# Lower limit and integer sums of a weight conversion moved from VectorE to GpSimd, first pair's phase 1 in other PSUM tiles, and a new order of left-over products

One core of one Trainium2 chip. The metric is the device time of one execution in microseconds (us); lower is better.

## The reference, cut

Cross attention between 8 x 512 tokens and 8 x 32 state rows, then a feed-forward layer with the gate h cos(h):

```python
def _moe_ref(x, w_in, w_out):          # x: 4352 x 512, w_in: 512 x 2048
    h = x @ w_in
    g = h * np.cos(h)
    return (g @ w_out).astype(np.float32)

def reference(**kwargs):               # ... cut: inputs split by name
    attn_out = _attn_ref(**attn_kwargs)        # softmax(x state^T) state, and back
    x = attn_out.transpose(0, 2, 1, 3).reshape(B * S, H * D)
    return _moe_ref(x=x, **moe_kwargs)
```

## The kernel before

The weights arrive as 64-bit floats. A load of 128 x 1024 values is rebuilt as 32-bit floats in parts named by letters: "1" and "2" on ScalarE, then the lower limit "a", the shift "b", the sign "c" and the integer sum "d".

```python
def convert_part(i, p):
    # ... cut: dst, bits (dst as int32), raw (64-bit source), e (low half)
    if p == "1":   nc.scalar.activation(dst, raw...[..., 1], func=ACTF.Abs)      # L206
    elif p == "2": nc.scalar.activation(e, raw...[..., 0], func=ACTF.Copy, ...)  # L209
    elif p == "a": nc.vector.tensor_scalar(dst, dst, 2.0 ** -15, None, op0=ALU.max)          # L212
    elif p == "b": nc.vector.tensor_scalar(bits, bits, 3, None, op0=ALU.logical_shift_left)  # L214
    elif p == "c": nc.vector.scalar_tensor_tensor(out=bits, in0=raw[..., 1], ...)            # L217
    else:
        engine = nc.vector if i < 4 else nc.gpsimd
        engine.tensor_tensor(bits, bits, e.bitcast(I32), op=ALU.add)                         # L223
```

The main loop has 144 steps of one hidden tile each; the first 128 belong to four pairs of batches, 32 steps to a pair, in four phases of eight. A step, cut:

```python
    hidden(t)                       # TensorE: h (L425)
    gate(t); gate2(t)               # ScalarE, then VectorE (L434)
    if conv >= 0: convert(conv, "1")
    # ... cut: attention work
    if conv >= 0: convert(conv, "a")
    gate3(t)                        # ScalarE: Abs, Sin
    gate4(t)                        # VectorE: h times cos(h), the gate product (L446)
    sums(t)                         # VectorE: subtractions for later products (L452)
    if conv >= 0: convert(conv, "2"); convert(conv, "bcd")
    output(line.pop(0))             # TensorE: products of the tile of three steps ago (L490)
```

A pair's output products are sums over eight tiles in one of two pairs of PSUM tiles, MAIN and SIDE (PSUM is the memory that TensorE's products are summed in). At the end of phase 2, MAIN is copied out by ScalarE (L501) and VectorE (L503); phase 3 begins with a new sum in MAIN, and TensorE may have to wait for the copies. That place is called a pair's jam below. The left-over products of the pair before (`more`) use SIDE and fill TensorE meanwhile. The weights s1 to s4 are sums and differences of blocks of `w_out`, made once by GpSimd; s2 and s4 stand for the products with them.

```python
        if t.phase == 3:
            if product(MAIN, s2, pr.b[0, i], i): ...   # wants MAIN at once
            free(pr.b[0, i])
            if product(SIDE, s4, t, i): ...            # wants SIDE
            free(t)
        elif pr.before and (t.phase * NH + i) % 3 < 2:
            pr.before.more(1)                          # 16 left-overs over phases 0 to 2
```

## Time and profile before

| | before |
|---|---|
| median of the first 3 executions | 836.75 us (834.78 to 836.91) |
| span of the profiled execution | 834.2 us |
| mean granted TensorE clock | 0.967 |

Two lines of the page of before, next to those that the prediction shows. In a profile, PE is TensorE's matmuls and PEld its weight loads, DVE is VectorE, ACT ScalarE and POOL GpSimd; the granted clock (PEclk) is the share of its full clock that TensorE was given. The first line has each engine's busy time, its share of the span and its number of instructions; the second line has GpSimd's busy tenths in 40 slices of about 21 us.

```profile
PE 775.2 (93%) x2720; PEld 349.1 (42%) x2720; DVE 463.3 (56%) x723; ACT 398.1 (48%) x644; POOL 99.4 (12%) x66
...
POOL 1033336776100000000000000000000000000200
```

GpSimd is busy 12% of the span, nearly all of it in the first eleven slices.

### The profile page before, as it was taken

What the parts mean: (1) busy time and instruction counts of PE and PEld (TensorE: products, weight loads), DVE (VectorE), ACT (ScalarE), POOL (GpSimd) and SP (SyncE); (2) the same over time, 40 slices, a digit from 0 to 9 for tenths busy, and PEclk for the clock granted to TensorE, in tenths of its full rate; (3) what the DMA queues carried; (4) which work ended last, traced back from release to release, by engine and by line L of the source; (5) the groups of instructions that cost most, each with busy time, mean ns of one, the idle gap of its engine ahead of it and who ended that gap; (6) DMA issues with size and microseconds to landing.
All of it is one profiled execution on the core that took longest, in us unless ns stands there. A gap on an engine that the chain in (4) does not pass through costs nothing.

```text
span 834.2 us, 7432 instructions
## 1 busy us (share of the span) xinstructions
PE 775.2 (93%) x2720; PEld 349.1 (42%) x2720; DVE 463.3 (56%) x723; ACT 398.1 (48%) x644; POOL 99.4 (12%) x66
## 2 busy tenths in 40 slices
PE   3589499989999999989999999899999999999997
PEld 2134144334434443434434344344444444355554
DVE  3889895662354446764455456853563455644331
ACT  1658775553437444634455445534363444322222
POOL 1033336776100000000000000000000000000200
PEclk9679989999999999989999999899999999999999
DMA  6584421102010211040011120130010110400121
GB/s 151 182 241 157 151 76 26 26 4 48 1 26 1 51 26 26 0 76 0 1 25 35 23 32 13 20 57 0 10 16 1 26 26 0 126 0 8 18 39 38
DMA packets 110500, 37.18 MB, mean 45 GB/s; under 512 B 102464, under 2 KB 102464, under 8 KB 110464
## 3 DMA queue, kind: packets, MB, share of 16 engines
q1 hardware_dynamic: 109248, 36.19, 18.6%
q10 hardware_dynamic: 1088, 0.26, 0.2%
q8 instruction: 21, 0.34, 0.2%
q0 software_dynamic: 128, 0.26, 0.2%
q14 instruction: 15, 0.12, 0.0%
HBM read 27.79 MB, written 8.91 MB: 44 GB/s over the span
## 4 chain that ended last, share of the span: by engine, by line
PE 76%; DVE 13%; ACT 7%; issue 1%; DMA 1%; POOL 0%; SPq 0%; DVEq 0%; POOLq 0%
PE o L490 41%; PE h L425 25%; PE at L277 4%; PE o L603 3%; DVE q L434 2%; ACT q L440 1%; DVE g_all L452 1%; DVE w_out L212 1%; PE at L250 1%; ACT q L439 1%; PE at L364 1%; DVE g_all L446 1%; DVE xT L297 1%; DMA x_b<-in_x_dram 1%; DVE w_out L217 1%
## 5 line engine op out<-in xcount | busy, mean ns | idle before, releaser
L425 PE MATMUL h<-aT,sw 128*128 128x512 f32 x512 | 247.0, 606 | 15.3 <-DVE g_all L446 9.4
L490 PE MATMUL o<-g_all,w_out 128*128 128x512 f32 x512 | 240.7, 606 | 9.8 <-ACT held L501 5.8
L431 ACT ACTIVATE q<-h 128x512 f32<-128x512 f32 (+1 forms) x144 | 82.4, 572 | 285.0 <-PE h L425 284.8
L434 DVE SCALAR_TENSOR_TENSOR q<-q,h 128x512 f32<-128x512 f32 (+1 forms) x144 | 94.4, 656 | 201.7 <-ACT q L431 201.6
L490 PE MATMUL o<-g_all,s 128*128 128x512 f32 x384 | 184.4, 616 | 8.2 <-ACT held L501 5.6
L446 DVE TENSOR_TENSOR g_all<-h,q 128x512 f32<-128x512 f32 (+1 forms) x144 | 94.9, 659 | 133.6 <-ACT q L440 133.4
L425 PEld LDWEIGHTS h<-aT,sw 128*128 128x128 f32 x512 | 98.9, 195 | 144.1 <-issue 115.5
L490 PEld LDWEIGHTS o<-g_all,w_out 128*128 128x128 f32 x512 | 94.7, 192 | 131.5 <-issue 122.3
L439 ACT ACTIVATE q<-q 128x512 f32<-128x512 f32 (+1 forms) x144 | 87.7, 609 | 103.2 <-DVE q L434 103.1
L490 PEld LDWEIGHTS o<-g_all,s 128*128 128x128 f32 x384 | 71.4, 195 | 102.9 <-issue 84.5
L440 ACT ACTIVATE q<-q,halfpi 128x512 f32<-128x512 f32 (+1 forms) x144 | 100.6, 699 | 4.5
L223 POOL TENSOR_TENSOR w_out<-w_out,s 128x1024 int32<-128x1024 int32 x10 | 23.6, 2359 | 603.9 <-DVE w_out L217 599.5
L452 DVE TENSOR_TENSOR g_all<-g_all 128x512 f32<-128x512 f32 x96 | 62.2, 688 | 1.6
L452 POOL TENSOR_TENSOR g_all<-g_all 128x512 f32<-128x512 f32 x32 | 40.0, 1276 | 26.2 <-DVE g_all L446 17.7
L425 PE MATMUL h<-sT,w_in 128*128 128x256 f32 x128 | 30.2, 379 | 0.0
L406 ACT COPY sw<-at 128x512 f32<-128x512 f32 x48 | 25.7, 589 | 9.0 <-PE at L277 9.0
L603 PE MATMUL o<-w_out,g_all 128*128 128x512 f32 x64 | 29.6, 592 | 0.0
L425 PEld LDWEIGHTS h<-sT,w_in 128*128 128x128 f32 x128 | 24.3, 190 | 10.1 <-issue 6.7
L496 DVE SCALAR_TENSOR_TENSOR held<-o,held 128x512 f32<-128x512 f32 x40 | 25.5, 682 | 4.3 <-PE o L490 4.3
L277 PE MATMUL at<-w_in,stT 64*32 64x512 f32 x384 | 26.1, 601 | 0.0
L517 DVE STREAM_TRANSPOSE ot<-held 128x512 f32<-128x512 f32 x32 | 22.3, 698 | 0.0
L223 POOL TENSOR_TENSOR w_in<-w_in,s 128x1024 int32<-128x1024 int32 x6 | 14.2, 2361 | 57.6 <-DVE w_in L217 57.6
(79 smaller groups left out, 456.1 us busy)
## 6 DMA issues: line engine op xcount, KB each, us to landing
out_dram<-ot SPq DMA_DIRECT2D x136, 64.0 KB, 2.0
x_b<-in_x_dram SPq DMA_DIRECT2D x32, 256.0 KB, 4.6
g_all<-in_moe_w_out_dram SPq DMA_DIRECT2D x8, 1024.0 KB, 5.0
g_all<-in_moe_w_in_dram SPq DMA_DIRECT2D x6, 1024.0 KB, 5.1
g_all<-in_moe_w_in_dram SPq DMA_DIRECT2D x4, 512.0 KB, 6.9
x_b<-in_moe_w_out_dram SPq DMA_DIRECT2D x1, 1024.0 KB, 6.0
xT<-in_moe_w_out_dram SPq DMA_DIRECT2D x1, 1024.0 KB, 8.1
s<-in_state_dram ACTq DMA_DIRECT2D x4, 64.0 KB, 5.3
```

The source lines that it names most:

```text
L223: engine.tensor_tensor(bits, bits, e.bitcast(I32), op=ALU.add)
L277: nc.tensor.matmul(out=(to or at)[j][Ns * k:Ns * k + Ns, 0:n], lhsT=w[D * j:D * j + D, self.b, Ns * k:Ns * k + Ns], rhs=r(slice(D * j, D * ...
L406: nc.scalar.copy(dst, to[j][:, 0:c1 - c0])
L425: nc.tensor.matmul(out=t.hp, lhsT=t.lhs(i), rhs=t.rhs(i), start=(i == 0), stop=(i == t.kn - 1))
L431: nc.scalar.activation(t.q, t.hp, func=ACTF.Copy, bias=MAGIC)
L434: nc.vector.scalar_tensor_tensor(out=t.q, in0=t.q, scalar=MAGIC, in1=t.hp, op0=ALU.subtract, op1=ALU.subtract)
L439: nc.scalar.activation(t.q, t.q, func=ACTF.Abs)
L440: nc.scalar.activation(t.q, t.q, func=ACTF.Sin, bias=halfpi, scale=-TWO_PI)
L446: nc.vector.tensor_tensor(t.g, t.hp, t.q, op=ALU.mult)
L452: engine.tensor_tensor(out, a, b, op=ALU.subtract)
L490: nc.tensor.matmul(out=acc[bank][ch], lhsT=w[:, i, P * ch:P * ch + P], rhs=g.g, start=(i == 0), stop=(i == NH - 1))
L603: nc.tensor.matmul(out=acc[MAIN][i], lhsT=t.g[:, P * i:P * i + P], rhs=w_out[:, :, t.f, :], start=(n == 0), stop=(n == NF - 1))
```

## The change

The intent is to relieve VectorE in the first 128 us, where it is full, and to shorten the waits of TensorE for PSUM at the start of phase 3. Three parts: (1) the lower limit and all integer sums go to GpSimd, which otherwise idles; (2) the first pair's phase 1 uses SIDE instead of MAIN, and the conversions are spread differently over the steps; (3) left-over products go first in a step and are spent earlier, and in phase 3 the product s4 (SIDE) goes ahead of s2 (MAIN).

```diff
         elif p == "a":
-            nc.vector.tensor_scalar(dst, dst, 2.0 ** -15, None, op0=ALU.max)
+            nc.gpsimd.tensor_scalar(dst, dst, 2.0 ** -15, None, op0=ALU.max)
...
-            engine = nc.vector if i < 4 else nc.gpsimd
-            engine.tensor_tensor(bits, bits, e.bitcast(I32), op=ALU.add)
+            nc.gpsimd.tensor_tensor(bits, bits, e.bitcast(I32), op=ALU.add)
...
+        if t.phase < 3 and pr.before and i % 3 < 2:
+            pr.before.more(1)
...
-            if product(MAIN, a12, t, i):
+            bank = MAIN if pr.before else SIDE
+            if product(bank, a12, t, i):
...
         if t.phase == 3:
-            if product(MAIN, s2, pr.b[0, i], i):
-            ... cut: sum with what is held
-            free(pr.b[0, i])
-            if product(SIDE, s4, t, i):
+            last = product(SIDE, s4, t, i)
+            free(t)
+            ... cut: sum with what is held
+            product(MAIN, s2, pr.b[0, i], i)
+            free(pr.b[0, i])
+            ... cut: sum with what is held
...
-        elif pr.before and (t.phase * NH + i) % 3 < 2:
-            pr.before.more(1)
...
-            prod(11, 0, 3, SIDE)
-            prod(13, 1, 0, SIDE)
+            prod(10, 0, 3, SIDE)
+            prod(13, 1, 0, MAIN)
...
-            prod(0, b, 1, *bank)
+            prod(0, b, 1, *[MAIN for _ in bank])
...
-    conv_at = {s: s + 4 for s in range(N_LOADS - 4)}
+    conv_at = {s: 4 + i for i, s in enumerate(
+        (0, 1, 2, 3, 4, 5, 6, 7, 8, 11, 12, 13, 14, 15))}
... cut: GpSimd's sums of weight blocks one or two steps later
```

More of the change, by code (lines that the diff above doesn't have):

```diff
@@ L574, in output @@
         if t.phase == 1:
-            if product(MAIN, a12, t, i):
+            bank = MAIN if pr.before else SIDE
+            if product(bank, a12, t, i):
                 o = Held()
                 for ch in range(2):
-                    plus(o, MAIN, ch, pr.u)
+                    plus(o, bank, ch, pr.u)
                 store(2 * pr.n, 0, o)
@@ L584, in output @@
         if t.phase == 3:
-            if product(MAIN, s2, pr.b[0, i], i):
-                for ch in range(2):
-                    plus(pr.u, MAIN, ch, pr.u)
-            free(pr.b[0, i])
-            if product(SIDE, s4, t, i):
+            last = product(SIDE, s4, t, i)
+            free(t)
+            if last:
                 o = Held()
@@ L592, in output @@
                     plus(o, SIDE, ch, pr.p5)
+            product(MAIN, s2, pr.b[0, i], i)
+            free(pr.b[0, i])
+            if last:
+                for ch in range(2):
+                    plus(pr.u, MAIN, ch, pr.u)
                 total(o, o, pr.u)
                 store(2 * pr.n + 1, 0, o)
-            free(t)
-        elif pr.before and (t.phase * NH + i) % 3 < 2:
-            pr.before.more(1)
     def state_output(t):
@@ L745 @@
     lo, hi = slice(0, NH // 2), slice(NH // 2, NH)
-    block_at = {13: (ALU.add, s1, a21, a22, lo),
-                15: (ALU.add, s1, a21, a22, hi),
-                17: (ALU.subtract, s2, s1, a11, lo),
-                18: (ALU.subtract, s2, s1, a11, hi),
-                19: (ALU.subtract, s4, a12, s2, lo),
-                20: (ALU.subtract, s4, a12, s2, hi),
+    block_at = {15: (ALU.add, s1, a21, a22, lo),
+                17: (ALU.add, s1, a21, a22, hi),
+                18: (ALU.subtract, s2, s1, a11, lo),
+                19: (ALU.subtract, s2, s1, a11, hi),
+                20: (ALU.subtract, s4, a12, s2, lo),
+                21: (ALU.subtract, s4, a12, s2, hi),
                 22: (ALU.subtract, s3, a11, a21, lo),
```

## The prediction

> **What bounds the kernel now.** I read the 40 slices first, for where TensorE is not full; then busy time in 20 us stretches, the groups by shape, the list of waits, and the timeline at each gap.
>
> ```profile
> PE   3589499989999999989999999899999999999997
> DVE  3889895662354446764455456853563455644331
> PEclk9679989999999999989999999899999999999999
> ...
> 80.00:100.00 20.00, 12.48 (x42) 4.58 (x40) 18.05 (x23) 13.74 (x20) 6.29 (x3) 1.00 0.41 143
> 100.00:120.00 20.00, 15.29 (x62) 6.70 (x63) 19.02 (x25) 16.24 (x23) 7.08 (x4) 0.74 0.29 104
> ```
>
> The columns of a stretch are PE, PEld, DVE, ACT, POOL, then clock, DMA share, GB/s. From about 128 us TensorE is full, with two dips (slices 17 and 26, 340-360 and 520-540 us) where the clock also falls. From 20 to 128 us VectorE is full instead: the weights arrive as 64-bit floats and are rebuilt there, one load a step. So only the first 128 us and the dips can yield; TensorE's matmuls themselves are not changed.
>
> ```profile
> L212 DVE TENSOR_SCALAR w_out<-w_out 128x1024 f32<-128x1024 f32 x10 | 16.0, 1598 | 1.9 <-ACT w_out L206 1.9
> L223 POOL TENSOR_TENSOR w_out<-w_out,s 128x1024 int32<-128x1024 int32 x10 | 23.6, 2359 | 603.9 <-DVE w_out L217 599.5
> L223 DVE CUSTOM_DVE_ANT_0 w_in<-w_in,s 128x1024 uint16<-128x1024 uint16 x4 | 2.8, 691 | 0.5 <-DVE w_in L217 0.2
> ...
> 80.33 0.65 DVE L212 TENSOR_SCALAR w_in<-w_in 128x1024 f32<-128x1024 f32 x1
> ...
> 118.41 2.37 POOL L223 TENSOR_TENSOR w_out<-w_out,s 128x1024 int32<-128x1024 int32 x1 [3.15 <-DVE w_out L217]
> 118.78 2.55 DVE L212 TENSOR_SCALAR w_out<-w_out 128x1024 f32<-128x1024 f32 x1
> ```
>
> The lower limit (L212) costs 0.65 us alone and 2.55 when the previous load's integer sum (L223) runs on GpSimd. A step without attention work takes 5.5 us (sums start at 72.00 and 77.53).
>
> ```profile
> PE o L490 <- ACT held L501: 11.4, 3, 5.8
> ...
> 104.05 2.05 PE L490 MATMUL o<-g_all,w_out 128*128 128x512 f32 x2 [5.80 <-ACT held L501]
> ...
> 352.54 1.28 DVE L496 SCALAR_TENSOR_TENSOR held<-o,held 128x512 f32<-128x512 f32 x2
> 356.85 2.08 PE L490 MATMUL o<-g_all,s 128*128 128x512 f32 x2 [2.79 <-ACT held L501]
> 358.40 0.68 DVE L503 TENSOR_SCALAR held<-o 128x512 f32<-128x512 f32 x1
> 359.14 4.78 PE L490 MATMUL o<-g_all,s 128*128 128x512 f32 x6 [0.21 <-DVE held L503]
> ```
>
> These three waits (the last column is the longest) are PSUM: a new sum wants the MAIN tiles before L501 and L503 copied the old one out. 104.05 is pair 0's phase 1, 356.85 pair 1's phase 3; the third (536.68) is pair 2's. Six matmul passes take 4.78 us here, 2.58 at full clock (0.43 each).
>
> **What the Trainium skill says.** "SBUF — State Buffer", section "Who interferes with whom": VectorE and GpSimd share a port pair under an exclusive lock, and a tensor_scalar in a 2-port mode waits for the whole GpSimd instruction. The trace agrees: L212 ends at 121.33, 0.55 after the sum's end at 120.78. "GPSIMD Engine Reference", section "Engine selection": two-input elementwise work is about twice as slow on GpSimd, one-input "roughly line-rate"; section "Elementwise — side-by-side cycle accounting" gives 1.03 cycles per element for a body that small. The first half agrees (512-wide subtraction 1.28 us on GpSimd, 0.69 on VectorE); the trace has no such one-input instruction of this size. "TensorE: Matmul & The Clock Gate", section "What's actually happening": half rate after an idle window of about 3.4 us. The trace agrees roughly: 2.8 us idle after 1.1 us of small matmuls halved the clock, gaps of 1.9 and 1.65 us (171.8, 712.3) did not.
>
> **Part 1, conversions.** VectorE loses 20 lower limits (16.0+7.2+1.6 = 24.8 us) and 4 sums (2.8); GpSimd gains them. Estimate of a GpSimd lower limit: 1024 x 1.03 / 1.2 GHz = 0.88 us plus 0.19 (the intercept of its sums: 1.276 at 512, 2.36 at 1024) = 1.07. The 24.8 us do not come off, because a loop forms: sum of load i, limit of i+1 (same in-order engine), shift, xor, sum of i+1. Its length: 2.36 + 1.07 + about 0.1 + 0.72 (shift start to xor start) + 1.36 (xor start to sum start, 70.64 to 72.00) = 5.6 us, against 5.5 now. So steps without attention gain nothing. Steps that VectorE's own sum sets do: shift to shift, load 11 came 7.44 us after load 10 (75.45 to 82.89) and becomes about 6.7; the next 6.71 minus 1.38 is below the loop, so 5.7. Start-up: the first sum is 0.6 us slower (1.28 for 0.69), but VectorE is freed of about 2 us ahead of the second softmax; I take -0.8.
>
> The conversions skip steps 9 and 10, and end in step 15 instead of 13. Steps 9 to 11 are set now by ScalarE's exponentials plus two conversions (gate products L446 at 87.81, 94.50, 102.43, 110.22). Without the latter: 8 to 9 about 4.8 (xor, then the chain L434, Abs, Sin, 2.1 us); 9 to 10 about 8 (the chain measured 7.62 at 336.58 to 344.20, plus the softmax sums); 10 to 11 about 4.5. That is 17.3 for 22.4. Then five loop steps at 5.7 end the last conversion near 130 us, where its sum started at 123.93 before, but the two 2.8 us steps that followed are now inside. Taken together, TensorE, which is full from 128.59 on, begins step 18's matmuls near 132.2 instead of 136.9: -4.4 us with start-up.
>
> **Part 2, first pair's phase 1 in SIDE.** It removes the 5.8 us wait at 104.05, but GpSimd, VectorE and ScalarE hold that stretch anyway: it is what lets part 1 show, and adds nothing to its sum.
>
> **Part 3, left-over products first, s4 before s2.** Nothing is added. Left-overs end at phase 2's fifth tile instead of its seventh, so L496 (1.28 us) leaves the jam before 356 us, and s4's four passes (1.72 us) stand between the old sum's end and the need for MAIN. Walking pair 1 with the measured durations: two of the left-overs come before step 56's matmuls that now come after, so step 55's gate is 1.7 us later, and with it the chain of 7.62 and 5.8 us behind it: the gate product of step 57 ends at 352.4 instead of 350.7. TensorE, now without filler, waits about 1.2 us for it, does the hidden matmuls (1.72) and the small ones (1.09), to 355.2, then s4 to 356.9. On VectorE the three subtractions after that gate product (1.9) run to 354.3 and L434 follows at once, with no L496 between; Abs, Sin and a copy later L501 ends near 357.6 (0.75 us of waiting), and L503, behind the next gate product and three subtractions, near 359.8 (1.3 us). The output step ends near 360.7 instead of 363.9 (359.14+4.78), with no idle stretch long enough to halve the clock: -3.2 each in pairs 1 and 2. Pair 3 (wait 1.65, no clock drop, fewer fillers): -0.5. Pair 0's gaps at 172-177 come from gates, unchanged. The phase order at a pair's start only exchanges which PSUM pair is drained first.
>
> Sum: 836.75 - 4.4 - 6.4 - 0.5 = 825.5. I add 1 for the risk in the GpSimd estimate: 826.5.
>
> **Rivals.** (a) GpSimd becomes the bound. If a limit takes 1.7 us, the loop is 6.2 and some nine loop steps lose 0.6 each: the early gain vanishes, about 830.5; at two-input speed (2.36) it turns to +6, about 836. For it: nothing of this kind is in the trace. Against it: the mask's one-input 128x128 instruction took 0.29 us there, so 0.1 over the intercept for 128 elements. (b) The jam only moves: with left-overs gone early, TensorE starves on the gates in phase 2 of every pair as much as it waited on L501, and the clock still halves. Then part 3 gives under 2 us: about 831. For it: VectorE is 64%, 94%, 99% and 83% busy in the four 5 us stretches from 340 to 360. (c) The early steps go better than the loop says, for example if the clock stays up between 100 and 112 us, where it was 0.5 to 0.7: about 820.
>
> **Range and chances.** (a) and (b) together reach 834, (c) with a full part 3 gives 819. Over 2% needs less than 820.0, which is (c): 0.1. Slower by 2% would need GpSimd far slower than any row shows: 0.02.
>
> **What would show it.** GpSimd's limits near 1.07 us at 1024 columns; no VectorE instruction of 2.5 us in the first 130; the sums 5.6-5.7 us apart in plain steps; the last of the first 14 near 130 us; no 5.8 us wait near 100; at phase 3, waits under 1.5 us and a clock of 1.0. A limit over 1.3 us, or slices 17 and 26 still with a clock below 1, would make it wrong.

## The result, and the profile after

| | before | after |
|---|---|---|
| median of 4 executions in the same rounds | 835.76 us (834.73 to 836.91) | 839.66 us (839.39 to 840.8) |
| span of the profiled execution | 834.2 us | 839.0 us |
| mean granted clock | 0.967 | 0.973 |

The ratio is 1.0049, with a 95% interval of 1.0029 to 1.0069. Here and below a ratio is the mean time of one kernel's fast executions over that of the other's in the same rounds, so not quite the ratio of the medians. The call "within 2%" held, but the time is outside the predicted range of 819 to 834, and on the other side of before.

The page of after, its busy line and four of its rows of slices:

```profile
PE 774.3 (92%) x2720; PEld 347.4 (41%) x2720; DVE 439.3 (52%) x699; ACT 397.8 (47%) x644; POOL 154.9 (18%) x90
...
PE   3469796989999999989999999999999999999997
...
DVE  2664766663236444786354446774564446643431
...
POOL 2677546967400000000000000000000000001300
PEclk9679988999999999999999999999999999999999
```

Two things are to be seen, one good and one bad. In slices 18 and 26, counted from 1, the clock is 9 where before had 8, and TensorE is 9 for 8 in slice 26: the jams at the start of phase 3 are mended in the main. (The first of these slices is the one that the prediction calls 17; it counted that one from 0 and the other from 1.) VectorE is at 6, 6 and 4 tenths in slices 2 to 4, where before had 8, 8 and 9, as intended. But TensorE is not higher for it: 4 and 6 for 5 and 8 in slices 2 and 3, and 6 for 9 in slice 7 (only slice 5 has 7 for 4). The time freed on VectorE isn't used. And GpSimd's busy time rose by 55.5 us, although VectorE's fell by only 24.0.

The stretch around pair 1's jam (340 to 400 us) shows the good part. Columns: length, then busy time and instructions of PE, PEld, DVE, ACT and POOL, then clock, DMA share and GB/s. First before, then after:

```profile
340.00:400.00 60.00, 56.99 (x205) 24.79 (x204) 37.13 (x61) 26.08 (x45) 0.00 (x0) 0.94 0.14 27
```

```profile
340.00:400.00 60.00, 57.52 (x206) 24.51 (x205) 44.18 (x73) 29.67 (x50) 0.00 (x0) 1.00 0.14 27
```

The clock is whole (1.00 for 0.94) in the stretch with the jam. Where exactly the time goes is best read by comparing one event per step. I took the start of every gate product on VectorE in both traces and subtracted. A step here is a turn of the main loop, counted from 0.

| gate product of step | before, us | after minus before, us |
|---|---|---|
| 4 | 63.19 | +4.70 |
| 18 | 141.57 | +12.08 |
| 40 | 259.18 | +11.95 |
| 64 (past pair 1's jam) | 392.29 | +8.99 |
| 96 (past pair 2's) | 572.65 | +5.51 |
| 128 (past pair 3's) | 739.33 | +4.82 |

So the kernel loses 12 us while the weights are converted and wins back 3.0, 3.5 and 0.7 us at the three jams. The loss is in the groups of after by shape (columns as in the prediction: busy us, mean ns, idle time before):

```profile
L211 POOL TENSOR_SCALAR w_out<-w_out 128x1024 f32<-128x1024 f32 x10 | 27.7, 2768 | 565.7 <-ACT w_out L205 565.7
L221 POOL TENSOR_TENSOR w_out<-w_out,s 128x1024 int32<-128x1024 int32 x10 | 23.6, 2356 | 21.7 <-DVE w_out L216 21.7
L213 DVE TENSOR_SCALAR w_out<-w_out 128x1024 int32<-128x1024 int32 x10 | 6.9, 693 | 17.1 <-POOL w_out L211 17.1
...
L211 POOL TENSOR_SCALAR w_in<-w_in 128x512 f32<-128x512 f32 x4 | 5.9, 1481 | 10.7 <-ACT w_in L205 10.7
```

The limit with its one input takes 2768 ns on GpSimd, longer than the sum with two inputs (2356), and VectorE's shift (L213) waits 17.1 us for it. One turn of the loop, from the timeline of after (start, duration, engine and line, then in brackets the idle time and its end):

```profile
42.11 2.36 POOL L221 TENSOR_TENSOR w_in<-w_in,s 128x1024 int32<-128x1024 int32 x1 [2.14 <-DVE w_in L216]
...
44.43 2.77 POOL L211 TENSOR_SCALAR w_in<-w_in 128x1024 f32<-128x1024 f32 x1
...
47.23 0.70 DVE L213 TENSOR_SCALAR w_in<-w_in 128x1024 int32<-128x1024 int32 x1 [2.54 <-POOL w_in L211]
...
47.97 1.23 DVE L216 SCALAR_TENSOR_TENSOR w_in<-g_all,w_in 128x1024 int32<-128x1024 int32 x1
...
49.34 2.37 POOL L221 TENSOR_TENSOR w_in<-w_in,s 128x1024 int32<-128x1024 int32 x1 [2.14 <-DVE w_in L216]
```

From sum to sum 7.23 us: sum to limit 2.32, limit to shift 2.80, shift to sign 0.74, sign to sum 1.37. Each releases the next, with nothing between. TensorE pays at the end, where it waits for the gate products that come behind:

```profile
136.41 3.78 PE L423 MATMUL h<-aT,sw 128*128 128x512 f32 x4 [5.53 <-DVE g_all L444]
```

### The profile page after: what moved, and what is told of

Its sections match the earlier page's. It is cut to its first block, busy times and chain, and to the rows that moved or that the text cites. A ratio compares the mean times of both kernels' runs of the same rounds, so it can differ in the third digit from the quotient of the medians.

```text
span 839.0 us, 7426 instructions
## 1 busy us (share of the span) xinstructions
PE 774.3 (92%) x2720; PEld 347.4 (41%) x2720; DVE 439.3 (52%) x699; ACT 397.8 (47%) x644; POOL 154.9 (18%) x90
## 4 chain that ended last, share of the span: by engine, by line
PE 73%; DVE 11%; POOL 8%; ACT 5%; DMA 1%; issue 1%; SPq 0%; POOLq 0%; DVEq 0%
PE o L488 40%; PE h L423 23%; PE at L275 3%; PE o L605 3%; POOL w_out L211 2%; DVE g_all L450 2%; POOL w_in L211 2%; POOL w_in L221 2%; POOL w_out L221 2%; DVE q L432 2%; ACT q L438 1%; PE at L248 1%; PE at L362 1%; DVE g_all L444 1%; DVE w_out L216 1%; ACT q L437 1%
## 5 line engine op out<-in xcount | busy, mean ns | idle before, releaser
L423 PE MATMUL h<-aT,sw 128*128 128x512 f32 x512 | 250.4, 613 | 23.3 <-DVE g_all L444 15.9
L488 PE MATMUL o<-g_all,s 128*128 128x512 f32 x384 | 178.7, 599 | 3.7 <-DVE held L501 3.7
L211 POOL TENSOR_SCALAR w_out<-w_out 128x1024 f32<-128x1024 f32 x10 | 27.7, 2768 | 565.7 <-ACT w_out L205 565.7
L221 POOL TENSOR_TENSOR w_out<-w_out,s 128x1024 int32<-128x1024 int32 x10 | 23.6, 2356 | 21.7 <-DVE w_out L216 21.7
L211 POOL TENSOR_SCALAR w_in<-w_in 128x1024 f32<-128x1024 f32 (+1 forms) x10 | 22.5, 2252 | 11.2 <-ACT w_in L205 11.2
```

The costliest lines, as they stand in the source:

```text
L211: nc.gpsimd.tensor_scalar(dst, dst, 2.0 ** -15, None, op0=ALU.max)
L221: nc.gpsimd.tensor_tensor(bits, bits, e.bitcast(I32), op=ALU.add)
L423: nc.tensor.matmul(out=t.hp, lhsT=t.lhs(i), rhs=t.rhs(i), start=(i == 0), stop=(i == t.kn - 1))
L488: nc.tensor.matmul(out=acc[bank][ch], lhsT=w[:, i, P * ch:P * ch + P], rhs=g.g, start=(i == 0), stop=(i == NH - 1))
```

## The experiments

The theory after the result: the one mis-sized term is the duration of the limit on GpSimd, and everything else in the prediction holds. Rivals: the whole transfer of work (the sums too) costs the time; the lock between VectorE and GpSimd that the prediction names costs it; part 2 or the order costs it; or the gain was never there, whatever the limit's speed. Fifteen kernels ran, all with results within tolerance. In the table, "early" is the gate product of step 18 and "jams" is what changed between steps 40 and 128, both against before's profiled execution. Kernels with identical code at the start differ there by up to 2 us from before, and by up to 2.9 us among themselves (the three that change only the order show -1.47, -1.98 and +0.87), so I read nothing from early differences below that.

| run | limit on | order | part 2 | median (before of same rounds) | ratio, 95% interval | early | jams |
|---|---|---|---|---|---|---|---|
| after | GpSimd | new | yes | 839.66 (835.76) | 1.0049, 1.0029 to 1.0069 | +12.08 | -7.13 |
| e1_limit_back | VectorE | new | yes | 828.35 (835.76) | 0.9911, 0.989 to 0.9932 | -1.54 | -7.12 |
| e3_order_alone | VectorE | new | no | 827.42 (835.76) | 0.9915, 0.989 to 0.994 | -1.47 | -7.13 |
| e4_part1_alone | GpSimd | old | no | 852.42 (835.76) | 1.0199, 1.018 to 1.0218 | +16.48 | -1.92 |
| e8_half_limit | half each | new | yes | 830.13 (834.82) | 0.9936, 0.9918 to 0.9954 | +1.37 | -7.12 |
| e13_copy_for_limit | GpSimd copy | new | yes | 823.92 (836.30) | 0.9853, 0.9831 to 0.9875 | -5.65 | -7.14 |
| e7_limit_late | VectorE, late | new | yes | 826.63 (834.82) | 0.9888, 0.9866 to 0.991 | -1.66 | -7.14 |
| e9_order_limit_late | VectorE, late | new | no | 830.44 (834.82) | 0.9937, 0.9918 to 0.9956 | +1.38 | -7.13 |
| e10_part2_alone | VectorE | old | yes | 833.21 (834.82) | 0.997, 0.9948 to 0.9993 | -1.86 | -0.15 |
| e5_leftovers_alone | VectorE | left-overs only | no | 837.15 (834.94) | 1.0018, 0.9997 to 1.0039 | +0.87 | +1.21 |
| e6_s4_alone | VectorE | s4 only | no | 825.93 (834.94) | 0.9894, 0.9866 to 0.9922 | -1.98 | -9.59 |
| e11_abc_early | VectorE | new | yes | 821.46 (834.94) | 0.9829, 0.981 to 0.9848 | -7.47 | -7.14 |
| e12_order_abc_early | VectorE | new | no | 820.83 (834.94) | 0.9828, 0.9812 to 0.9844 | -7.82 | -7.14 |
| e14_s4_abc_early | VectorE | s4 only | no | 821.02 (836.30) | 0.9822, 0.9803 to 0.984 | -7.78 | -8.04 |
| e15_s4_part2_abc_early | VectorE | s4 only | yes | 820.09 (836.30) | 0.9811, 0.9793 to 0.9828 | -8.44 | -7.96 |

### Taking the limit out of part 1, and part 1 by itself

e1 is after with one line back; e4 is before with part 1 only; e3 is before with part 3 only.

```diff
--- after.py
+++ e1_limit_back
-            nc.gpsimd.tensor_scalar(dst, dst, 2.0 ** -15, None, op0=ALU.max)
+            nc.vector.tensor_scalar(dst, dst, 2.0 ** -15, None, op0=ALU.max)
--- before.py
+++ e4_part1_alone
-            nc.vector.tensor_scalar(dst, dst, 2.0 ** -15, None, op0=ALU.max)
+            nc.gpsimd.tensor_scalar(dst, dst, 2.0 ** -15, None, op0=ALU.max)
-            engine = nc.vector if i < 4 else nc.gpsimd
-            engine.tensor_tensor(bits, bits, e.bitcast(I32), op=ALU.add)
+            nc.gpsimd.tensor_tensor(bits, bits, e.bitcast(I32), op=ALU.add)
```

e3 takes over the new place of `more` and the new phase 3 from the change's diff, with `bank = MAIN`.

> The changed kernel with only the lower limits back on VectorE (the four first sums stay on GpSimd). Theory: the 12 us lost before step 18 come back, perhaps 2 to 4 us more because the two conversions that are left out of steps 9 and 10 now show, and the 7 us won at the phase changes stay: 823 to 829 us. Rival (moved schedule at fault): still above 836.

> The kernel before with only the lower limits and the first four integer sums moved to GpSimd. Theory (a GpSimd limit takes 2.77 us of 1024 columns, so that limit, shift, xor and sum form a loop of 2.36 + 2.77 + 0.1 + 0.72 + 1.36 = 7.3 us per load): the first 14 conversion steps take about 7.2 us each, so 9 to 13 us are lost before step 18 and nothing is won later: 845 to 849 us. Rival (the early loss comes from the moved schedule of conversions and block sums, not from the limit): within 2 us of before, 834 to 838.

> The kernel before with only the order of products changed (left-over products first in a phase, s4 before s2). Theory: the waits at the change from phase 2 to phase 3 in pairs 1 and 2 shrink and the clock stays at 1.0 there, -3.0 and -3.5 us, and -0.7 in pair 3: 828 to 830 us. Rival (the smaller gaps in the changed kernel come from something else, such as its later start): 834 to 837.

One line back on VectorE turns +3.9 us into -7.4 (828.35 for 835.76): the limit alone is worth 11.3 us of after. The sums stayed on GpSimd in e1, and e1 and e3 are alike in both columns, so the sums and part 2 together cost nothing there; nor does one hide the other, as part 2 without the sums (e10 below) comes as early at step 18 (-1.86 for -1.54). e4 lost 16.7 us by the medians, even more than expected; its profiled execution, the fastest of the four at 850.50, is 16.5 us behind at step 18 and wins 1.9 back at the jams. e3 gives the value of part 3 by itself: about 8 us, of which 7.1 at the jams.

### The limit's duration, measured by itself

p1 is before with a row of GpSimd instructions behind the last step in the program, on tiles that nothing needs any more (dead tiles), and not in place; its time means nothing. Most of them ran while the last steps were still under way.

```diff
+    for _ in range(4):
+        nc.gpsimd.tensor_scalar(to, src, 2.0 ** -15, None, op0=ALU.max)
+    # ... cut: the same with op0=ALU.mult, ALU.add; tensor_copy(to, src);
+    # tensor_tensor(to, src, oth) with mult, add; max of 512 columns;
+    # and four limits on VectorE
```

> The kernel before with a row of GpSimd instructions of 128x1024 behind it, on dead tiles, out of place, four of each: limit (max), times a constant, plus a constant, copy, product of two tiles, sum of two tiles, limit at 512 columns; and the limit on VectorE. Theory (tensor_scalar on GpSimd is slow by itself, whatever its operation): 2.77 us for all three with a constant, 1.48 at 512 columns, 2.36 for two tiles, copy unknown. Rival 1 (only max is slow): constant product and sum near 1.1. Rival 2 (the 2.77 us are a wait for VectorE's lock on the shared port, or in-place use): the limit takes near 1.1 here. The result is right, the time means nothing.

Its lines in the probe's profile, in this order; after the count they have the lowest, median and highest duration in ns, then the first and last start:

```profile
L813 POOL TENSOR_SCALAR s<-s x4: 2765/2766/2777, 787.6 to 796.2; 128x1024 f32<-128x1024 f32 x4
L815 POOL TENSOR_SCALAR s<-s x4: 2770/2770/2775, 799.0 to 807.6; 128x1024 f32<-128x1024 f32 x4
L817 POOL TENSOR_SCALAR s<-s x4: 2769/2770/2776, 810.4 to 819.0; 128x1024 f32<-128x1024 f32 x4
L819 POOL COPY s<-s x4: 1039/1211/1381, 821.8 to 825.5; 128x1024 f32<-128x1024 f32 x4
...
L823 POOL TENSOR_TENSOR s<-s x4: 2338/2339/2340, 837.2 to 844.5; 128x1024 f32<-128x1024 f32 x4
L825 POOL TENSOR_SCALAR s<-s x4: 1485/1486/1492, 846.9 to 851.6; 128x512 f32<-128x512 f32 x4
```

It is neither the operation (max, times and plus a constant all take 2.77 us) nor work in place. Nor is it VectorE's company: the limit of p1 at 790.46 us had no VectorE instruction beside it at all and took 2.77 us, and after's 16 limits of this size took 2.76 to 2.78 us with 0.24 to 2.73 us of VectorE's work beside them. (Company can add to it: one limit of e4, at 117.17 us, took 3.74 us.) A copy with the same bytes takes 1.04 us at its lowest (the two of 1.38 us ran beside VectorE's probe instructions). From 512 to 1024 columns a limit grows by 2766 - 1486 = 1280 ns, so 2.5 ns a column.

### Changing the limit's duration

e8 gives half of each limit to VectorE, so that GpSimd's takes 1.48 us (VectorE's half runs beside it: 0.74 us at 49.53, with GpSimd's from 49.38 to 50.86). e13 puts the copy in the limit's place: wrong, as the limit is missing (with this data the result still passes), to get an instruction of almost the duration that the prediction assumed, with the same waits.

```diff
--- after.py
+++ e8_half_limit
-            nc.gpsimd.tensor_scalar(dst, dst, 2.0 ** -15, None, op0=ALU.max)
+            # ... cut: lo_ and hi_ are the two halves of dst
+            nc.gpsimd.tensor_scalar(lo_, lo_, 2.0 ** -15, None, op0=ALU.max)
+        elif p == "h":                       # ahead of "b" at every place
+            nc.vector.tensor_scalar(hi_, hi_, 2.0 ** -15, None, op0=ALU.max)
--- after.py
+++ e13_copy_for_limit
-            nc.gpsimd.tensor_scalar(dst, dst, 2.0 ** -15, None, op0=ALU.max)
+            nc.gpsimd.tensor_copy(dst, dst)
```

> The changed kernel with half of each lower limit on GpSimd (512 columns, 1.48 us) and the other half on VectorE (about 0.36 us, just ahead of the shift, so that the shared port makes it wait for GpSimd's half). Theory: the loop per load falls from 7.3 to about 6.4 us and, with some ten plain steps, 8 to 11 us of the early loss come back: 829 to 832 us, sums in plain steps 6.3 to 6.5 us apart. Rival (VectorE's waits for the lock are the cost, not the length of the loop): no better than the changed kernel, 838 or more, as there is one more instruction that waits for the lock.

> The changed kernel with an in-place copy on GpSimd (1.04 to 1.2 us of 1024 columns in the row of single instructions) in place of each lower limit: the result may be wrong for very small weights, on purpose. Theory (only the limit's time was wrong in the prediction): the loop is 2.36 + 1.04 + 0.1 + 0.72 + 1.36 = 5.6 us, step 18's gate product comes 2 to 5 us earlier than in the kernel before instead of 12 later, 823 to 828 us. Rival (a second error: VectorE's waits for the port and the gate chain eat what is left): step 18 no earlier than before, 829 to 832.

Two turns of the loop in the timeline of e13:

```profile
110.13 2.37 POOL L221 TENSOR_TENSOR w_out<-w_out,s 128x1024 int32<-128x1024 int32 x1 [2.13 <-DVE w_out L216]
...
112.44 1.04 POOL L211 COPY w_out<-w_out 128x1024 f32<-128x1024 f32 x1
...
113.52 0.69 DVE L213 TENSOR_SCALAR w_out<-w_out 128x1024 int32<-128x1024 int32 x1 [0.79 <-POOL w_out L211]
...
115.61 2.36 POOL L221 TENSOR_TENSOR w_out<-w_out,s 128x1024 int32<-128x1024 int32 x1 [2.13 <-DVE w_out L216]
```

The sums are 5.48 us apart, where the prediction had 5.6. With 1.04, 1.48 and 2.77 us in the limit's place, sums in plain steps are 5.48, 5.98 (e8: 47.05 to 53.02) and 7.23 us apart, so a step pays for the limit in full; step 18 comes -5.65, +1.37 and +12.08 us against before. Between the ends that is 17.7 us, some ten such steps. (Half way it is not in proportion: 7.0 us for the first 0.44, of which ten steps make 5.) The time with 1.04 us is 823.92, within 2 us of the prediction's sum of 825.5. That settles the cause: the arithmetic stood, the duration put into it did not.

### Does the lock cost anything?

In before, a limit takes up to 2.55 us because GpSimd's sum runs at the same time. e7 undoes part 1 and moves the limit behind the gate product, where that sum has ended; e9 does the same without part 2.

```diff
--- after.py, with part 1 undone (e7), and also part 2 (e9)
-        if conv >= 0:
-            convert(conv, "a")
         gate3(t)
...
-            convert(conv, "bcd")
+            convert(conv, "abcd")
```

> The changed kernel with part 1 undone (limits and first four sums on VectorE) and each lower limit placed behind the step's gate product instead of ahead of it, so that the previous load's sum on GpSimd is over by then. Theory (the 2.5 us limits are waits for the lock): every limit takes 0.65 us, plain steps shrink from 5.5 to about 5.2, and steps with attention by their whole wait: 4 to 9 us under the kernel with the limit ahead of it (828.4), so 819 to 824. Rival (the chain of gate and xor sets these steps, not the wait): 826 to 829.

> The kernel before with the order of products changed and each lower limit behind the gate product; the PSUM tiles and the schedule of conversions as before. Theory (part 2 gains nothing alone because the two conversions left out of steps 9 and 10 come back in steps 14 and 15): within 1.5 us of the same kernel with part 2, 819 to 825. Rival (part 2 is worth the 5.8 us wait that it removes): 5 us above it.

Two lines of e7's timeline:

```profile
74.02 0.69 DVE L445 TENSOR_TENSOR g_all<-h,q 128x512 f32<-128x512 f32 x1 [1.45 <-ACT q L439]
74.63 0.68 DVE L211 TENSOR_SCALAR w_in<-w_in 128x1024 f32<-128x1024 f32 x1
```

My expectation of e7 fell. Every limit of 1024 columns takes 0.68 to 0.69 us, as wanted, yet plain steps take 5.32 us (sums at 72.12 and 77.44) for 5.53 before, and the time is level with e1 and e3. The waits under the lock were filling time that was there anyway, as VectorE then stands 1.45 us waiting for the sine, and the limit now follows behind it. The step is set by the chain gate, Abs, Sin, gate product, then limit, shift, sign. e9 missed too (830.44 for 819 to 825): between it and e7, part 2 is worth 3.8 us.

Part 2 by itself:

```diff
--- before.py
+++ e10_part2_alone      # ... cut: the other lines of part 2 from the diff above
-            if product(MAIN, a12, t, i):
+            bank = MAIN if pr.before else SIDE
+            if product(bank, a12, t, i):
```

> The kernel before with only the first pair's second phase in the other PSUM tiles, with its schedule of conversions and block sums; limits and sums as before. Theory: the wait of 5.8 us at 104 us goes, the gate products of steps 11 to 13 come about 5 us earlier, and the conversions in steps 14 and 15 take it back: 834 to 836.5. Rival: 830 to 831.

The gain is small (833.21 for 834.82; the interval of the ratio allows 0.6 to 4.3 us). The 5.8 us wait is gone and gate products of steps 11 to 13 come some 4.5 us earlier, but the conversions that were put off to steps 14 and 15 give most of it back: step 18 is 1.9 us earlier, no more than the noise.

### Putting the waiting time to use

If the chain of e7 is right, the gain lies in moving shift and sign ahead of the gate product, into VectorE's wait for the sine. e11 is after with part 1 undone, e12 is before with the new order only, both with:

```diff
-        if "c" in parts and i + 3 < N_LOADS:
+        if "d" in parts and i + 3 < N_LOADS:      # where the next load is fetched
...
-            convert(conv, "a")
+            convert(conv, "abc")
...
-            convert(conv, "bcd")
+            convert(conv, "d")
```

> The changed kernel with part 1 undone (limits and first four sums on VectorE), and limit, shift and xor all ahead of the gate product, in the 1.45 us that VectorE waits for ScalarE's sine. Theory (the chain gate, Abs, Sin, product, shift, xor sets plain steps at 5.2 to 5.5 us): without shift and xor behind the product a plain step is 0.65 + 1.1 (rest of the sum on GpSimd) + 0.65 + 0.7 + 1.2 + 0.65 = 4.9 us; 3 to 6 us under the kernel with part 1 undone and the limit behind the product (826.6): 820.5 to 823.5. Rival (the early steps are set by ScalarE or by VectorE's sum of work): 826 to 828.

> The kernel before with the order of products changed and limit, shift and xor ahead of the gate product, without part 2. Theory: the same shortening of plain steps, but two conversions still fall in steps 9 and 10, which ScalarE's exponentials set, so less is won: 822 to 827. Rival: as the kernel with the order alone, 827 to 829.

From the timeline of e11:

```profile
67.08 2.38 POOL L222 TENSOR_TENSOR w_out<-w_out,s 128x1024 int32<-128x1024 int32 x1 [2.69 <-DVE w_out L216]
...
68.64 1.36 DVE L211 TENSOR_SCALAR w_in<-w_in 128x1024 f32<-128x1024 f32 x1
...
72.14 2.37 POOL L222 TENSOR_TENSOR w_in<-w_in,s 128x1024 int32<-128x1024 int32 x1 [2.69 <-DVE w_in L216]
```

Here the limit waits for the lock again (1.36 us for 0.68) and yet a step takes 5.06 us. VectorE now has no idle time from one gate product (66.85) to the next (71.91), so here the lock's 0.68 us may well cost something; no run tests that. The gain by step 18 is 7.5 us, with every instruction of the conversion on the engine where before had it. Plain steps, 0.26 us shorter than in e7, give little of it; more comes from steps with attention work (gate products of steps 3 and 4 are 5.67 us apart for 7.05 in e7). e12 without part 2 is as fast as e11.

### Part 3 taken apart

e5 has only the new place of `more`, e6 only s4 ahead of s2.

```diff
--- before.py
+++ e5_leftovers_alone
+        if t.phase < 3 and pr.before and i % 3 < 2:
+            pr.before.more(1)
...
-        elif pr.before and (t.phase * NH + i) % 3 < 2:
-            pr.before.more(1)
--- before.py
+++ e6_s4_alone
-            if product(MAIN, s2, pr.b[0, i], i): ...
-            free(pr.b[0, i])
-            if product(SIDE, s4, t, i): ...
+            last = product(SIDE, s4, t, i)
+            free(t)
+            ... cut
+            product(MAIN, s2, pr.b[0, i], i)
+            free(pr.b[0, i])
```

> The kernel before with only the left-over products put first in a phase (and so done by the third phase's fifth tile), s2 still ahead of s4 in the last phase. Theory (both halves of the order are needed: this one takes the two adds of the left-overs out of the jam, s4 gives time for the copy of the old sum): TensorE reaches the jam earlier and still waits for the copy, the clock still falls: 833 to 837. Rival (the left-overs alone do it): 828 to 830.

> The kernel before with only s4 ahead of s2 in the last phase. Theory: 1.7 us of products stand ahead of the wait for the copied sum, which in pairs 1 and 2 came 2.8 us late, so about 1 us of waiting is left for the first tile, some for the second, and the clock perhaps stays up: -1.5 to -4 us in pairs 1 and 2 each: 828 to 833. Rival (s4 needs the SIDE tiles, which the left-overs' adds hold until 353.8 us, so nothing is won): 834 to 837.

Pair 1's jam in the timelines of after, e5 and e6, in this order:

```profile
364.60 1.98 PE L423 MATMUL h<-aT,sw 128*128 128x512 f32 x4 [1.32 <-DVE g_all L444]
...
367.53 3.10 PE L488 MATMUL o<-g_all,s 128*128 128x512 f32 x6
...
371.80 1.12 PE L488 MATMUL o<-g_all,s 128*128 128x512 f32 x2 [1.16 <-DVE held L501]
```

```profile
353.52 1.98 PE L425 MATMUL h<-aT,sw 128*128 128x512 f32 x4 [1.33 <-DVE g_all L446]
...
358.44 1.12 PE L490 MATMUL o<-g_all,s 128*128 128x512 f32 x2 [1.91 <-ACT held L501]
...
360.73 4.30 PE L490 MATMUL o<-g_all,s 128*128 128x512 f32 x6 [1.16 <-DVE held L503]
```

```profile
351.88 1.99 PE L490 MATMUL o<-g_all,s 128*128 128x512 f32 x4
...
354.74 1.12 PE L490 MATMUL o<-g_all,s 128*128 128x512 f32 x2 [0.87 <-ACT held L501]
...
357.03 1.12 PE L490 MATMUL o<-g_all,s 128*128 128x512 f32 x2 [1.16 <-DVE held L503]
```

With the left-overs earlier but s2 still first (e5), TensorE first stands 1.33 us for lack of them and then 1.91 and 1.16 us for PSUM; six matmuls then take 4.30 us, at a granted clock of 0.66 from 360 to 365 us, and nothing is gained (837.15 for 834.94). The prediction read from before that gaps of 1.9 us leave the clock whole; e5, where no wait at this jam is longer, shows that this does not always hold. With s4 first and the left-overs where they were (e6), the wait of 1.3 us for the gate product is not there, the two waits for PSUM are 0.87 and 1.16 us with matmuls at full clock, and the jams give 9.6 us, more than both together (7.1). In these traces the new place of the left-overs takes back part of what s4 wins. The times don't separate the two: e6's four executions fall in two groups, 824.25 and 824.28 (the profiled one), 827.59 and 827.65, and its ratio interval overlaps with e3's.

### Combining

e14 is e6 with the early conversion of e12, e15 adds part 2.

```diff
--- before.py
+++ e14_s4_abc_early       # the diff of e6 and that of e11
+++ e15_s4_part2_abc_early # the same and that of e10
```

> The kernel before with s4 ahead of s2, and limit, shift and xor on VectorE ahead of the gate product; left-overs in the order of before, no part 2. Theory (s4 alone wins 9.6 us and the left-overs first cost 2.4 of them): 2 to 3 us under the kernel with both orders and the early limit, shift and xor (820.8): 818 to 819. Rival (equal within noise): 820 to 822.

> The same with part 2's PSUM tiles and schedule. Theory (part 2 moves two conversions from steps that ScalarE sets to steps that nothing else fills, and wins nothing in sum): within 1 us of the one without, 817.5 to 819.5. Rival (part 2 shows once the conversions are short): 815 to 817.

e14 missed: 821.02 where I expected 818 to 819, and no better than e12. Its jams give 8.0 us, not the 9.6 that e6 had. The whole difference lies at pair 2 (-2.64 for -4.20 us), where e14 has the same two waits as e6, 0.87 and 1.16 us, but a granted clock of 0.83 from 525 to 535 us, where e6 has 1.00. Why the clock fell in the one and not in the other is not shown. e15 is the lowest of all at 820.09 (ratio 0.9811 [0.9793, 0.9828]), but 0.9 us under e14 is within their ranges: that part 2 helps there is not shown.

## Why the prediction was wrong, point by point

**The failed step: the size of one term.** "Estimate of a GpSimd lower limit: 1024 x 1.03 / 1.2 GHz = 0.88 us plus 0.19 [...] = 1.07." Measured: 2.77 us. The prediction's term is 1.70 us too short, in a sum where every loop step pays it. The loop becomes 2.36 + 2.77 + 0.1 + 0.72 + 1.36 = 7.31 us; measured, 7.23. With the prediction's own nine loop steps, 9 x 1.70 = 15.3 us turns its -4.4 into +10.9 and its sum into 840.8; measured by step 18 is +12.1, and 839.66 as the time. The trace had no such instruction, and the prediction said so; it should have let the range follow from that. The check that it offered, the mask's instruction of 128 columns at 0.29 us, was another operation (an affine select) and no stand-in: a line through the limit's 1.48 us at 512 and 2.77 at 1024 columns has the intercept that was assumed, 0.19, but makes 0.51 us at 128. The intercept was right, the slope was three times the assumed one.

**Rival (a) named the cause, but stopped short.** It said "GpSimd becomes the bound", and at 2.36 us "about 836". The limit was slower than the worst case it allowed. Its sums were loose besides: at 2.36 us, nine steps of 1.29 us each turn the -4.4 into +7.2 and the time into 837, and even its own 836 lay outside the range, which ended at 834. "A limit over 1.3 us" as what would make it wrong was right.

**The mechanism was right.** The loop sum, limit, shift, sign, sum sets plain steps (each released by the one before it, and e13 with 5.48 us for 5.6 predicted). Moving 24 us of busy time off VectorE could not shorten it. The last of the first 14 conversions' sums starts at 146.22 us, 22 us later than before; the prediction had the conversion end near 130. In e13, with a limit's stand-in of the predicted length, that sum runs from 127.69 to 130.06, and steps 8 to 11, which the prediction put at 17.3 us, take 18.0.

**Part 2 "adds nothing to its sum".** Alone it gives 1.6 us by the medians (e10), which fits. But it is worth more beside other changes: 3.8 us between e9 and e7. With part 1 there is no direct pair of runs; from e4's +16.5 and after's +12.1 by step 18 it is some 4 us.

**Part 3: right in size, half right in reason, so the size is partly luck.** Predicted -3.2, -3.2 and -0.5; measured -3.0, -3.5 and -0.7, with the clock at 1.0. Rival (b), that TensorE starves on the gates as much as it waited before, is refuted: it waits 1.32 us for them, where it had waited 2.79 for PSUM. The predicted wait of "about 1.2 us" for lack of filler is there (1.32), and the wait of 1.3 us for L503 too (1.16); that of 0.75 for L501 is not. But the prediction also credited the left-overs' new place with taking L496 out of the jam. e5 shows that this by itself wins nothing, and e6 that s4 first does all of it, with L496 still there (at 350.42).

**Rival (c)**, an early part better than the loop allows, did not come with this change; e11 and e12 reach it in another way.

What stays open: why part 2 is worth 4 us in some settings (e9 and e7) and nothing in others (e12 and e11), and what makes the clock fall at one jam and not at another with the same waits. The second question bears on e4 too, which has the order of before and still gains 1.9 us at the jams: at pair 1 TensorE waits 2.78 us as before (2.79), but the clock is 0.83 over the ten microseconds around it (370 to 380), where before has 0.66 (355 to 365).

## What to carry to other kernels

Before work moves to another engine, measure that very instruction there, in its size, on dead data at the end of a kernel: one such run would have changed this prediction by 15 us. A loop over several engines is priced by the sum of its links, so an engine that is 18% busy over the span, as GpSimd is in after, can still be the one that a step waits for. And before work is moved to another engine at all, look whether the full engine has a wait inside its own step: moving shift and sign into VectorE's 1.45 us wait for the sine won 5.9 us by step 18 in e11 against e1 and 6.4 in e12 against e3, where moving the limit away lost 12.

## What the Trainium skill lacked or had wrong

- "GPSIMD Engine Reference", section "Engine selection", calls one-input elementwise work on GpSimd "roughly line-rate". Here only a plain copy came near that (1.04 us at 128 x 1024). A tensor_scalar with max, mult or add took 2.77 us, about 2.66 times as long, and longer than a tensor_tensor of two inputs (2.34).
- The same page, section "Elementwise — side-by-side cycle accounting", gives 1.03 cycles per element for a body as small as a limit's. The slope measured is 2.5 ns a column (1.48 us at 512, 2.77 at 1024); at the 1.2 GHz of its section "Specifications" this is 3.0 cycles. No page says that tensor_scalar is a case of its own on GpSimd.
- "SBUF — State Buffer", section "Who interferes with whom", says that a tensor_scalar in a 2-port mode waits for the whole of a GpSimd instruction that was issued first. The trace agrees, and shows that size is no protection: the addition of a constant to 128 x 2 values took 2.01 us on VectorE (at 132.13 in after), beside GpSimd's sum from 131.76 to 134.11. What no page says is when such waits cost anything: e7 removed them from the limits, and a plain step went from 5.53 to 5.32 us only, as the time was filled by VectorE's wait for the sine.
